# A 16-bit pass moved to GpSimd when it is idle, and the choice of blocks for VectorE, in a scheduled attention kernel

## The chip, the cores and the metric

The kernel runs on one core of one Trainium2 chip. The metric is device time in microseconds of one execution; lower is better. The core has five engines that run their own instruction lists and wait for each other by semaphores: TensorE (PE, matrix products), ScalarE (ACT, here above all exponentials), VectorE (DVE, elementwise work), GpSimd (POOL, elementwise work, no access to PSUM, the accumulators' memory) and SyncE (SP, which issues DMA transfers). SBUF is the core's working memory.

## The reference: what is computed

Four layers work on x, 2048 positions of 512 numbers, each adding its result to x after a layer norm: attention (A), linear attention (B), A, B.

```python
# A: 32 query heads of 16, one key and one value head for all
q = heads(x @ wq); k = x @ wk; v = x @ wv
p = softmax(q k^T * 16**-0.5)
x = x + merge(p v) @ wo
# B: 32 heads of 16, phi(t) = (t + 1 if t > 0 else exp(t)) + 1e-6
kv = sum_s phi(k) v ; z = sum_s phi(k)
x = x + merge(phi(q) kv / (phi(q) z + 1e-6)) @ wo
```

In an A layer the costly part is the exponential of 32 x 2048 x 2048 scores.

## The kernel before

**Blocks.** Scores are made in blocks of 128 keys by 512 columns (128 queries of four heads). A *segment* (class `Seg`, L294) is a query tile `t` (of 16), one of two parities `par`, and a list of key tiles `kts`; it has four blocks (`j` = 0 to 3) for each key tile. The segments of tiles 0 to 3 come in several pieces of few key tiles (`a_segs`, L736); those of tiles 4 to 15 are whole: 16 key tiles, 64 blocks, 24 segments to a layer. A layer has 2048 blocks in all. QK matmuls (L782) write a block's scores to a PSUM bank; the products with V (L836, "PV") add up in one other bank, with four blocks of different `j` side by side; at the end of a segment VectorE copies or adds that bank to `sacc` (L1068, L1070), and `norm` (L1077) transposes and divides it.

**Two ways to the exponential.** ScalarE does most blocks, in groups of two or three (L948, PSUM to `PT`). VectorE does others without an exponential: it adds a constant and writes the result as a 16-bit integer whose bits, read as bfloat16, are near a power of two (L1024, `dve_take`, PSUM to a buffer of `FB`). The first such write alone is coarse, so `NSH` = 4 shifted versions are used, with weights: up to `CHB` = 4 blocks are gathered in one `FB` buffer, a *chunk*, and `dve_shifts` (L1041) makes three further copies with a 16-bit integer added (L1049, SBUF to SBUF, 2048 elements a partition), each in a buffer of its own. PV takes all four, so a block of VectorE's needs four PV matmuls in place of one.

**Who chooses.** `act_stream` (L888) builds ScalarE's groups one after another. For each it asks `dve_split` (the third bank of a group goes to VectorE) or `dve_open` (a free bank goes there). These say no when VectorE's queue is long (`BLS`, `BLO`, `BLT`) or, for a new chunk, when no more than `FBO` = 2 of the `NFB` = 10 buffers are free (`dve_hit`, L996). `dve_pick` (L980) then looks through the running segment and the next four for a block: one of a segment is taken only when more than `CHT` = 12 blocks are left from the running segment up to it (in the last segment `ENDL` = 12) and when more than the share 1 - `DMAX` of its own blocks, one half, is left. `stale` (L975) closes a chunk early when its segment is past or has `CHT // 2` blocks left. `dve_shifts` holds passes of far segments back when few buffers are free (`FBS`, `AHEAD`).

**The order of the work** is written by a planner in Python before the launch (class `Planner`, L36). Each operation has a duration by engine, keys that it reads and writes, and a priority (lower goes first). When an engine is free in the planner's own time, `_dispatch1` (L127) gives it the ready operation with the lowest number; this fixes each engine's instruction list. `backlog` (L104) is the planned time in an engine's queue. `emit` (L274) writes the lists out with semaphore waits for the keys. Thus the durations used for planning shape the order, and on the chip each engine goes through its list in that order, however long things take.

**Others that the change touches.** `ln_tile` (L620) makes the layer norm: statistics on VectorE, `rs` = 1/sqrt on GpSimd (L630), `xn` on VectorE (L633), then a transpose by TensorE or by DMA. `phi` (L1168) makes phi for B layers on ScalarE (L1170) and VectorE (L1171, L1173); its keys go to `pk`, a tile of its own (L398), which `kv_` (L1244) reads. `fill` (L862) and `fill_lin` (L764) put dummy matmuls where TensorE would stand still (L881, L768). `mode` of an operation tells how the TensorE array is split: rows (QK), columns (PV), or full.

Of the kernel before, what the change touches and what calls it, by code (L numbers as in the profile page):

```python
# [6 lines left out]
BF16 = mybir.dt.bfloat16  # L7
# [16 lines left out]


class Op:
    __slots__ = ("eng", "opts", "fn", "deps", "prio", "left", "users", "done", "end", "n", "value", "sem", "signal", "isdma", "name", "freed", "begun", "slot", "cols", "mode")


class Pool_:  # L30
# [5 lines left out]
class Planner:  # L36
# [3 lines left out]
    def __init__(self, nc):  # L40
        self.nc = nc
        self.now = 0.0
        self.events = []
        self.seq = 0
        self.ready = {e: [] for e in ENGS}
        self.busy = {e: False for e in ENGS}
        self.until = {e: 0.0 for e in ENGS}
        self.order = {e: [] for e in ENGS}
        self.writer = {}
        self.readers = {}  # L50
        self.flags = {}
        self.flagwait = {}
        self.level = (0.0, 0.0)
        self.due = []
        self.idle = []
        self.mode = None

    def at(self, t, fn):
        self.seq += 1
# [2 lines left out]
    def ws(self, k):  # L62
        return self.writer.get(k, [])

    def op(self, opts, reads=(), writes=(), prio=5.0, lat=0.08, dma=False, name="", join=None, mode="full"):

        o = Op()
        o.opts, o.prio, o.users, o.done, o.end = opts, prio, [], False, None
        o.eng, o.fn, o.n, o.value, o.sem, o.signal, o.isdma = None, None, None, None, None, False, dma
        o.name = (name, lat)  # L70
        o.freed = False
        o.begun = None
        o.cols = 0
        o.mode = mode
        deps = set()
        for k in reads:
            deps.update(self.ws(k))
        for k in writes:
# [11 lines left out]
        for k in reads:  # L90
# [36 lines left out]
    def _dispatch1(self, e):  # L127
        if self.busy[e]:
            return
        h = self.ready[e]  # L130
        while h:
            _, _, o = heapq.heappop(h)
            if o.eng is not None:
                continue
            dur, fn = o.opts[e]
            if e == PE:
                if self.mode != o.mode:
                    dur += SWITCH
                self.mode = o.mode
            o.eng, o.fn = e, fn  # L140
            self.order[e].append(o)
            self.busy[e] = True
            self.until[e] = self.now + dur
# [6 lines left out]
            return  # L150

    def _freed(self, e, o):
        self.busy[e] = False
# [171 lines left out]
MCRIT = {0: (), 1: (0, 1), 2: (), 3: ()}  # L325
ECRIT = (15,)
WORK = 5000
DMAX = 0.5
RING = 24
NOB = 4  # L330
DTL = 4.0
# [28 lines left out]
CHB = 4  # L360
FBO = 2
FBS = 4
AHEAD = 20
CHT = 12


def bass_interleave_layers__grouped_kv_mqa__linear_attn_block__prompt_kernel(
# [11 lines left out]
    pl = Planner(nc)  # L379
    op = pl.op  # L380
    sb = nc.alloc_sbuf_tensor
# [13 lines left out]
    wo = sb("wo", [P, 4, D], BF16)  # L395
    wqkv = sb("wqkv", [P, FT, 3 * D], BF16)
    wo2 = sb("wo2", [P, 4, D], BF16)
    pk = sb("pk", [P, 8, D], BF16)  # L398
    va = sb("va", [P, 8, H * 17], BF16)
    NXN = 6  # L400
    xn = sb("xn", [P, NXN, D], BF16)
    st = sb("st", [P, T, 2, 6], FP32)
    mv = sb("mv", [P, T, 2], FP32)
    ve = sb("ve", [P, T], FP32)
    rs = sb("rs", [P, T], FP32)
    mhalf = sb("mhalf", [P, 1], FP32)
# [9 lines left out]
    zz = sb("zz", [P, 128], BF16)  # L416
    NPT = 6
    PT = sb("PT", [P, NPT, GA * 512], BF16)
    NFB = 10
    FB = sb("FB", [P, NFB, CHB * 512], BF16)  # L420
    NOS, NOT = 3, 2
    Osb = sb("Osb", [P, NOS, D], BF16)
    OT = sb("OT", [P, NOT, 4, P], BF16)
    rden = sb("rden", [P, 2, 16], FP32)
    sacc = sb("sacc", [P, 8, 512], FP32)
    NAS = 2
    identF = sb("identF", [P, P], FP32)
    NPH = 3
    phE = sb("phE", [P, NPH, D], BF16)
# [47 lines left out]
    def B_(i):  # L477
        return ("bank", i)
# [141 lines left out]
    def ln_tile(t, prio, far=False, crit=False):  # L620
        if t in two:
            two.discard(t)
            n = 2
        else:
            n = 1
# [2 lines left out]
        op({DV: (0.07, lambda e: e.tensor_scalar(out=ve[:, t:t + 1], in0=mv[:, t, 1:2], scalar1=1e-5, scalar2=None, op0=ALU.add))},  # L628
           reads=[("mv", t)], writes=[("ve", t)], prio=prio, lat=0.16)
        op({PO: (0.55, lambda e: e.tensor_tensor(out=rs[:, t:t + 1], in0=ve[:, t:t + 1], in1=mhalf[:], op=ALU.pow))},  # L630
           reads=[("ve", t), "mhalf"], writes=[("rs", t)], prio=prio)
        i = yield ("acq", xn_pool, prio)
        op({DV: (0.325, lambda e: e.tensor_scalar(out=xn[:, i, :], in0=x_sb[:, t, :], scalar1=mv[:, t, 0:1], scalar2=rs[:, t:t + 1],  # L633
                                                op0=ALU.subtract, op1=ALU.mult))},
           reads=[("x", t), ("mv", t), ("rs", t)], writes=[("xn", i)], prio=prio)
        if far:
            o = dmat(xnT[:, :, t * P:(t + 1) * P], xn[:, i, :], [("xn", i)], [("xnT", t)], prio)
            pl.give_after(xn_pool, i, [o])
# [133 lines left out]

    def run_a(L):
        segs = a_segs()
        state = {"si": 0, "done": False, "on": False}

        def qk_reads(sg, kts):
            return [("QT", sg.t)] + [("K", sg.par, kt) for kt in kts]
# [262 lines left out]
        def dve_shifts(blk, f_, hold):  # L1041
            n = 512 * len(blk)
            pr = 8.0 + 0.001 * min(x[0].i for x in blk)
            si = min(x[0].i for x in blk)
            for w in range(1, NSH):
                while len(fb_pool.free) <= FBS and sum(x.total - x.submitted for x in segs[cur["i"]:si]) > (AHEAD if segs[si].blocks < 32 else 0):
                    yield ("sleep", 0.2)
                g_ = yield ("acq", fb_pool, pr)
                o = op({DV: (n / 3840.0 + 0.066, lambda e, w=w, g_=g_: e.tensor_scalar(  # L1049
                    out=FB[:, g_, 0:n].bitcast(I16), in0=FB[:, f_, 0:n].bitcast(I16), scalar1=float(w * 128 // NSH), scalar2=None, op0=ALU.add))},  # L1050
                       reads=[("FB", f_, h) for h in range(len(blk))], writes=[("FB", g_, h) for h in range(len(blk))], prio=pr, lat=0.15)
# [112 lines left out]
    def run_b(L):  # L1164
        def base(t):
            return 1.0 if t >= CRIT else 5.0

        def phi(b, dst, key, pr, n=D, join=None):  # L1168
            i = yield ("acq", ph_pool, pr)
            op({AC: (0.07 + n / 1200.0, lambda e: e.activation(phE[:, i, 0:n], bank(b, n), ACTF.Exp))}, reads=[B_(b)], writes=[("phE", i)], prio=min(pr, 0.9))  # L1170
            op({DV: (0.07 + n / 3840.0, lambda e: e.tensor_scalar(out=phE[:, i, 0:n], in0=phE[:, i, 0:n], scalar1=1.0, scalar2=1e-6, op0=ALU.min, op1=ALU.add))},  # L1171
               writes=[("phE", i)], prio=pr)
            o = op({DV: (0.07 + n / 960.0, lambda e: e.scalar_tensor_tensor(out=dst, in0=bank(b, n), scalar=0.0, in1=phE[:, i, 0:n], op0=ALU.max, op1=ALU.add))},  # L1173
                   reads=[("phE", i)], writes=[B_(b), key], prio=pr, join=join)
            pl.give_after(banks, b, [o])
            pl.give_after(ph_pool, i, [o])
            return o

        def phi_k(t, b, sl, pr):
            yield from phi(b, pk[:, sl, :], ("pk", sl), pr)  # L1180
            pl.flag(("pkin", L, t))

        def crit_k(t, sl, pr):
            bs = yield from acq2(pr)
            for h in range(2):
                mm(bank(bs[h], 256), [(xnT[:, ft, t * P:(t + 1) * P], wqkv[:, ft, D + h * 256:D + h * 256 + 256]) for ft in range(FT)],
                   [("xnT", t), "wqkv"], bs[h], pr + 0.0001 * h, 0.45)
            o = None
            for h in range(2):
                o = yield from phi(bs[h], pk[:, sl, h * 256:h * 256 + 256], ("pk", sl), pr, 256, o)  # L1190
            pl.flag(("pkin", L, t))

        def crit_v(t, sl, pr):
# [50 lines left out]
        def kv_(gi, ts):  # L1244
            pr = base(ts[-1]) + 0.01 * ts[-1] + 0.005
            end = gi == len(KVG) - 1
# [15 lines left out]
            for gs in ((0, 1, 2), (3,)):  # L1262
# [6 lines left out]
                def fn(e, gs=gs, b=b):  # L1269
# [3 lines left out]
                            ins = e.matmul(ps[:, b * 512 + i * 136:b * 512 + (i + 1) * 136], lhsT=pk[:, t % 8, g * P:(g + 1) * P],  # L1273
                                           rhs=va[:, t % 8, g * 136:(g + 1) * 136], start=(not end and t == ts[0]), stop=(t == ts[-1]), skip_group_check=True)
                    return ins
                rd = [("pk", t % 8) for t in ts] + [("va", t % 8) for t in ts]
                o = op({PE: (0.08 * len(gs) * len(ts), fn)}, reads=rd, writes=[B_(b)], prio=pr, lat=0.2)
                o.cols = 136 * len(gs) * len(ts)
                dst = kvacc[:, gs[0] * 136:gs[0] * 136 + n]
# [197 lines left out]
```

## Time and profile before

| what | value |
|---|---|
| time, median of three runs (lowest, highest) | 1580.71 us (1577.74, 1581.18) |
| the profiled execution: its own time | 1583.91 us |
| its span in the profile | 1582.0 us |
| busy: PE, DVE, ACT, POOL | 1474.2, 1372.0, 1509.3, 62.9 us |
| blocks by VectorE (L1024) | 924 of 4096 |
| passes of 2048 elements (L1049) | 693 |
| granted TensorE clock, mean | 0.995 |

The profile is one execution on the chip. A line of a group gives the source line, engine, operation, tiles (out<-in), shapes and count, then busy time in us, mean ns of one, idle time of the engine before them and what ended it ("releaser"). Instructions of an engine overlap a little, so the busy time is less than count times mean. In a timeline a line gives the start and the length in us of a row of like instructions.

### The profile page before, as it was taken

The page shows a single profiled execution, that of the slowest core. Times are in us where ns is not written, and L with a number is a line of the kernel's source. Part 1 is how long each engine was busy: PE and PEld are TensorE (multiplying, and loading weights), DVE is VectorE, ACT ScalarE, POOL GpSimd, SP SyncE. Part 2 cuts the span into 40 slices and gives each one's busy share as a digit, 9 for nine tenths or more (in the row PEclk, how much of TensorE's full clock was granted, in tenths as well). Part 3 has the DMA queues.
Part 4 walks back from the last instruction along what each step waited for, and adds up shares of the span by engine and source line. Part 5 has one row for each costly group of instructions (what it writes and reads, how often), then busy time and mean ns, then how long its engine had stood idle before and what let it go on. Part 6 is the DMA issues. An engine that isn't in the chain of part 4 may idle for free.

```text
span 1582.0 us, 35711 instructions
## 1 busy us (share of the span) xinstructions
PE 1474.2 (93%) x14564; PEld 546.7 (35%) x14667; DVE 1372.0 (87%) x2550; ACT 1509.3 (95%) x1481; POOL 62.9 (4%) x122
## 2 busy tenths in 40 slices
PE   8998999999999999999999999999999999999989
PEld 4432332333333333332644323323333333333335
DVE  7799899999898989997566789999889898998957
ACT  7999999999999999999599999999999999999982
POOL 4000000000000000000011000000000000000000
PEclk9999999999999999999999999999999999999999
DMA  5100000000000000000000000000000000000001
GB/s 128 48 2 1 12 11 12 5 9 7 8 8 8 5 8 5 1 2 1 2 1 1 1 2 15 15 8 8 5 5 8 8 8 8 8 1 2 1 2 54
DMA packets 40433, 17.52 MB, mean 11 GB/s; under 512 B 34128, under 2 KB 39760, under 8 KB 40272
## 3 DMA queue, kind: packets, MB, share of 16 engines
q1 hardware_dynamic: 40272, 15.25, 4.1%
q8 instruction: 117, 1.92, 0.5%
q14 instruction: 44, 0.36, 0.1%
HBM read 5.28 MB, written 2.10 MB: 5 GB/s over the span
## 4 chain that ended last, share of the span: by engine, by line
PE 42%; ACT 36%; DVE 11%; issue 10%; DMA 0%; POOL 0%; SPq 0%; ACTq 0%; DVEq 0%; POOLq 0%
ACT PT L948 35%; PE ps L836 14%; PE ps L782 12%; DVE FB L1024 5%; PE ps L550 4%; PE ps L881 4%; DVE FB L1049 2%; PE ps L707 2%; PE ps L1087 2%; ACT phE L1170 1%; PE ps L768 1%; DVE sacc L1068 1%; DVE st L626 0%; PE ps L1400 0%; PE ps L1381 0%
## 5 line engine op out<-in xcount | busy, mean ns | idle before, releaser
L948 ACT ACTIVATE PT<-ps 128x1024 bf16<-128x1024 f32 (+1 forms) x1350 | 1460.1, 1216 | 13.0 <-PE ps L836 7.2
L1024 DVE TENSOR_SCALAR FB<-ps 128x512 int16<-128x512 f32 x924 | 617.0, 685 | 92.9 <-PE ps L782 88.6
L782 PE MATMUL ps<-QT,KM 32*128 32x512 bf16 x4096 | 529.7, 385 | 51.2 <-ACT PT L948 32.8
L836 PE MATMUL ps<-PT,V 128*32 128x512 bf16 x3172 | 463.5, 388 | 20.3 <-ACT PT L948 17.1
L1049 DVE TENSOR_SCALAR FB<-FB 128x2048 int16<-128x2048 int16 x693 | 451.2, 681 | 2.3 <-PE ps L836 0.5
L836 PE MATMUL ps<-FB,VW 128*32 128x512 bf16 x3696 | 411.1, 384 | 15.7 <-DVE sacc L1068 5.2
L782 PEld LDWEIGHTS ps<-QT,KM 32*128 32x128 bf16 x4096 | 137.9, 91 | 425.4 <-ACT PT L948 188.8
L881 PE MATMUL ps<-QT,V 128*32 128x512 bf16 (+6 forms) x786 | 178.3, 315 | 0.5 <-issue 0.3
L836 PEld LDWEIGHTS ps<-PT,V 128*32 128x32 bf16 x3172 | 116.4, 94 | 156.1 <-ACT PT L948 70.6
L836 PEld LDWEIGHTS ps<-FB,VW 128*32 128x32 bf16 x3696 | 108.6, 94 | 178.2 <-issue 86.3
L630 POOL TENSOR_TENSOR rs<-ve,mhalf 128x1 f32<-128x1 f32 x64 | 45.7, 723 | 1422.3 <-DVE ve L628 1386.0
L881 PEld LDWEIGHTS ps<-QT,V 128*32 128x32 bf16 x786 | 58.9, 95 | 82.0 <-issue 59.6
L550 PE MATMUL ps<-wqkv,xnT 128*128 128x512 bf16 (+1 forms) x218 | 68.1, 369 | 3.0 <-issue 2.1
L1087 PE MATMUL ps<-identF,sacc 128*128 128x128 f32 x256 | 48.6, 293 | 2.9 <-DVE sacc L1068 1.7
L1068 DVE COPY sacc<-ps 128x512 f32<-128x512 f32 x64 | 43.7, 683 | 7.8 <-PE ps L836 7.8
L1170 ACT ACTIVATE phE<-ps 128x512 bf16<-128x512 f32 (+1 forms) x66 | 41.3, 625 | 5.3 <-PE ps L707 3.6
L626 DVE BATCH_NORM_STATS2 st<-x_sb 128x6 f32<-128x512 bf16 x60 | 40.6, 678 | 3.3 <-DMA x_sb<-in_A_x_dram 3.1
L1070 DVE TENSOR_TENSOR sacc<-sacc,ps 128x512 f32<-128x512 f32 x56 | 38.2, 683 | 5.6 <-PE ps L836 4.7
L707 PE MATMUL ps<-xnT,wqkv 128*128 128x128 bf16 x512 | 42.2, 221 | 0.0
L707 PE MATMUL ps<-xnT,wq 128*128 128x128 bf16 x480 | 40.8, 226 | 0.6 <-DMA wq<-in_A_wq_dram 0.6
L550 PEld LDWEIGHTS ps<-wqkv,xnT 128*128 128x128 bf16 x272 | 21.8, 96 | 46.1 <-issue 38.4
L1087 PEld LDWEIGHTS ps<-identF,sacc 128*128 128x128 f32 x256 | 27.4, 140 | 27.4 <-issue 11.1
(114 smaller groups left out, 673.5 us busy)
## 6 DMA issues: line engine op xcount, KB each, us to landing
out_dram<-x_sb SPq DMA_DIRECT2D x16, 128.0 KB, 1.7
x_sb<-in_A_x_dram SPq DMA_DIRECT2D x3, 512.0 KB, 6.9
wqkv<-in_B_wqkv_dram SPq DMA_DIRECT2D x1, 1536.0 KB, 7.3
xnT<-xn SPq DMA_TRANSPOSE x36, 2.4
x_sb<-in_A_x_dram SPq DMA_DIRECT2D x4, 128.0 KB, 2.2
wq<-in_A_wq_dram SPq DMA_DIRECT2D x1, 512.0 KB, 5.0
wo<-in_A_wo_dram SPq DMA_DIRECT2D x1, 512.0 KB, 4.0
wo<-in_B_wo_dram SPq DMA_DIRECT2D x1, 512.0 KB, 8.4
```

The lines of the kernel that those rows point to most:

```text
L550: return e.matmul(dst, lhsT=l, rhs=r, start=(k == 0), stop=(k == len(pairs) - 1))
L630: op({PO: (0.55, lambda e: e.tensor_tensor(out=rs[:, t:t + 1], in0=ve[:, t:t + 1], in1=mhalf[:], op=ALU.pow))}, reads=[("ve", t), "mhalf"] ...
L707: ins = e.matmul(dst[:, g * P:(g + 1) * P], lhsT=lhs(g, k), rhs=rhs(k), start=(k == 0), stop=(k == FT - 1))
L782: return e.matmul(bank(b), lhsT=KM[r, sg.par, kt * P:(kt + 1) * P], rhs=QT[r, sg.t, :], start=True, stop=True)
L836: ins = e.matmul(ps[32 * j:32 * j + 32, ACC * 512:(ACC + 1) * 512], lhsT=V[:, kt, :] if w is None else VW[:, kt, w, :], rhs=ap, start=(k = ...
L881: o = op({PE: (n / 2400.0, lambda e: e.matmul(ps[32 * j:32 * j + 32, b * 512:b * 512 + n], lhsT=V0[:], rhs=QT[:, sg.t, 0:n], start=st, sto ...
L948: ex = op({AC: (0.05 + 0.4267 * n, lambda e, n=n, s_=s_, p_=p_: e.activation(PT[:, p_, 0:n * 512], ps[:, s_ * 512:(s_ + n) * 512], ACTF.Ex ...
L1024: o = op({DV: (0.60, lambda e: e.tensor_scalar(out=dst.bitcast(I16), in0=bank(b), scalar1=VB, scalar2=VLO, op0=ALU.add, op1=ALU.max))}, wr ...
L1049: o = op({DV: (n / 3840.0 + 0.066, lambda e, w=w, g_=g_: e.tensor_scalar(out=FB[:, g_, 0:n].bitcast(I16), in0=FB[:, f_, 0:n].bitcast(I16), ...
L1068: o = op({DV: (0.6, lambda e, src=src: e.tensor_copy(src, bank(ACC)))}, writes=[B_(ACC), key], prio=0.0, lat=0.15)
L1087: o = op({PE: (0.12, lambda e, c=c: e.transpose(ps[:, b * 512 + c * P:b * 512 + (c + 1) * P], src[:, c * P:(c + 1) * P], identF[:]))}, rea ...
L1170: op({AC: (0.07 + n / 1200.0, lambda e: e.activation(phE[:, i, 0:n], bank(b, n), ACTF.Exp))}, reads=[B_(b)], writes=[("phE", i)], prio=min ...
```

## The change

Four things are changed together.

First, an operation can be marked `port`: VectorE's passes (L1049), its `xn` and the first step of `phi` carry the mark, and so does a pass on GpSimd. In the planner, no marked operation starts while another one runs; the engine takes something else from its queue in the meantime. Second, a pass of a full chunk may go to GpSimd: when GpSimd is idle, no other such pass is under way, and VectorE's planned queue is over `PBL` = 0.6 us. While the queue is that long, `dve_shifts` waits for the chunk's last eviction before it decides. `rs` gets a higher priority on GpSimd. Third, `DMAX` goes from 0.5 to 1.0 and `CHT` from 12 to 20, and `FB` has 12 buffers in place of 10; the room comes from `pk`, which now lies in `sacc[2:6]`, with the dependencies for that. Fourth, TensorE, when it would change between columns and full array, goes on with an operation of the present mode if one is ready within `STICK` = 1.5 of the priority.

```diff
-DMAX = 0.5
+DMAX = 1.0
-CHT = 12
+CHT = 20
+PSH = True
+STICK = 1.5
+PBL = 0.6
-    pk = sb("pk", [P, 8, D], BF16)
-    NFB = 10
+    NFB = 12
     sacc = sb("sacc", [P, 8, 512], FP32)
+    pk = sacc[:, 2:6, :].rearrange("p a b -> p (a b)").bitcast(BF16).rearrange("p (s d) -> p s d", d=D)
...
@@ Planner._dispatch1
         while h:
-            _, _, o = heapq.heappop(h)
+            x = heapq.heappop(h)
+            o = x[2]
             if o.eng is not None:
                 continue
             dur, fn = o.opts[e]
+            if o.port and self.port > self.now:
+                held.append(x)
+                continue
+            if e == PE and STICK and o.mode != "row" and o.mode != self.mode != "row":
+                like = [y for y in h if y[2].eng is None and y[2].mode == self.mode and y[0] <= o.prio + STICK]
+                if like:
+                    y = min(like)
+                    h.remove(y)
+                    heapq.heapify(h)
+                    held.append(x)
+                    o = y[2]
+                    dur, fn = o.opts[e]
+            if o.port:
+                self.port = self.now + dur
...
+        for x in held:
+            heapq.heappush(h, x)
+        if held and not self.busy[e] and e != PE:
+            self.at(self.port, lambda: self._dispatch(e))
...
@@ ln_tile: rs, then xn
-           reads=[("ve", t), "mhalf"], writes=[("rs", t)], prio=prio)
+           reads=[("ve", t), "mhalf"], writes=[("rs", t)], prio=prio - 9.0)
...
-           reads=[("x", t), ("mv", t), ("rs", t)], writes=[("xn", i)], prio=prio)
+           reads=[("x", t), ("mv", t), ("rs", t)], writes=[("xn", i)], prio=prio, port=True)
...
@@ dve_shifts
                 g_ = yield ("acq", fb_pool, pr)
-                o = op({DV: (n / 3840.0 + 0.066, lambda e, w=w, g_=g_: e.tensor_scalar(
+                while PSH and len(blk) == CHB and pl.backlog(DV) > PBL and not all(o.done for o in pl.ws(("FB", f_, len(blk) - 1))):
+                    yield ("sleep", 0.1)
+                pool = PSH and len(blk) == CHB and not pl.busy[PO] and state["po"] == 0 and pl.backlog(DV) > PBL
+                if pool:
+                    state["po"] += 1
+                en, du = (PO, n / 1165.0 + 0.25) if pool else (DV, n / 3840.0 + 0.066)
+                o = op({en: (du, lambda e, w=w, g_=g_: e.tensor_scalar(
                     out=FB[:, g_, 0:n].bitcast(I16), in0=FB[:, f_, 0:n].bitcast(I16), scalar1=float(w * 128 // NSH), scalar2=None, op0=ALU.add))},
-                       reads=[("FB", f_, h) for h in range(len(blk))], writes=[("FB", g_, h) for h in range(len(blk))], prio=pr, lat=0.15)
+                       reads=[("FB", f_, h) for h in range(len(blk))], writes=[("FB", g_, h) for h in range(len(blk))], prio=pr, lat=0.15, port=True)
+                if pool:
+                    def gone():
+                        state["po"] -= 1
+                    o.users.append(gone)
...
@@ phi, kv_
-            o = op({DV: (0.07 + n / 960.0, ...)}, reads=[("phE", i)], writes=[B_(b), key], prio=pr, join=join)
+            o = op({DV: (0.07 + n / 960.0, ...)}, reads=[("phE", i)], writes=[B_(b), key], prio=pr, join=join, after=after)
...
-            yield from phi(b, pk[:, sl, :], ("pk", sl), pr)
+            yield from phi(b, pk[:, sl, :], ("pk", sl), pr, after=[("sacc", 2 + sl // 2)])
...
-                rd = [("pk", t % 8) for t in ts] + [("va", t % 8) for t in ts]
+                rd = [("pk", t % 8) for t in ts] + [("va", t % 8) for t in ts] + [("sacc", u) for u in sorted({2 + t % 8 // 2 for t in ts})]
```

The new argument `after` of an operation lists keys that it must come behind, with their readers and writers, without writing them.

More of the change, by code (lines that the diff above doesn't have):

```diff
@@ L26 @@
 class Op:
-    __slots__ = ("eng", "opts", "fn", "deps", "prio", "left", "users", "done", "end", "n", "value", "sem", "signal", "isdma", "name", "freed", "begun", "slot", "cols", "mode")
+    __slots__ = ("eng", "opts", "fn", "deps", "prio", "left", "users", "done", "end", "n", "value", "sem", "signal", "isdma", "name", "freed", "begun", "slot", "cols", "mode", "port")
 class Pool_:
@@ L56, in __init__ @@
         self.mode = None
+        self.port = 0.0
     def at(self, t, fn):
@@ L63, in ws, with op @@
         return self.writer.get(k, [])
-    def op(self, opts, reads=(), writes=(), prio=5.0, lat=0.08, dma=False, name="", join=None, mode="full"):
+    def op(self, opts, reads=(), writes=(), prio=5.0, lat=0.08, dma=False, name="", join=None, mode="full", port=False, after=()):
         o = Op()
@@ L74, in op @@
         o.mode = mode
+        o.port = port
         deps = set()
@@ L77, in op @@
             deps.update(self.ws(k))
-        for k in writes:
+        for k in list(writes) + list(after):
             deps.update(self.ws(k))
@@ L89, in op @@
                 self.readers[k] = []
-        for k in reads:
+        for k in list(reads) + list(after):
             if k not in writes:
@@ L130, in _dispatch1 @@
         h = self.ready[e]
+        held = []
         while h:
-            _, _, o = heapq.heappop(h)
+            x = heapq.heappop(h)
+            o = x[2]
             if o.eng is not None:
@@ L149, in _dispatch1 @@
             self.at(self.now + dur + o.name[1], lambda: self._done(o))
-            return
+            break
+        for x in held:
+            heapq.heappush(h, x)
+        if held and not self.busy[e] and e != PE:
+            self.at(self.port, lambda: self._dispatch(e))
     def _freed(self, e, o):
@@ L774, in run_a @@
         segs = a_segs()
-        state = {"si": 0, "done": False, "on": False}
+        state = {"po": 0, "si": 0, "done": False, "on": False}
         def qk_reads(sg, kts):
@@ L1166, in base, with phi @@
             return 1.0 if t >= CRIT else 5.0
-        def phi(b, dst, key, pr, n=D, join=None):
+        def phi(b, dst, key, pr, n=D, join=None, after=()):
             i = yield ("acq", ph_pool, pr)
@@ L1171, in phi @@
             op({DV: (0.07 + n / 3840.0, lambda e: e.tensor_scalar(out=phE[:, i, 0:n], in0=phE[:, i, 0:n], scalar1=1.0, scalar2=1e-6, op0=ALU.min, op1=ALU.add))},
-               writes=[("phE", i)], prio=pr)
+               writes=[("phE", i)], prio=pr, port=True)
             o = op({DV: (0.07 + n / 960.0, lambda e: e.scalar_tensor_tensor(out=dst, in0=bank(b, n), scalar=0.0, in1=phE[:, i, 0:n], op0=ALU.max, op1=ALU.add))},
-                   reads=[("phE", i)], writes=[B_(b), key], prio=pr, join=join)
+                   reads=[("phE", i)], writes=[B_(b), key], prio=pr, join=join, after=after)
             pl.give_after(banks, b, [o])
@@ L1189, in crit_k @@
             for h in range(2):
-                o = yield from phi(bs[h], pk[:, sl, h * 256:h * 256 + 256], ("pk", sl), pr, 256, o)
+                o = yield from phi(bs[h], pk[:, sl, h * 256:h * 256 + 256], ("pk", sl), pr, 256, o, [("sacc", 2 + sl // 2)])
             pl.flag(("pkin", L, t))
```

## The prediction

> **What bounds the kernel now.** I first read the table by stretches, cut where the costliest groups change. Columns: stretch and length, then busy time and instruction count of PE, its weight loads, VectorE, ScalarE and GpSimd, then TensorE's granted clock.
>
> ```profile
> 80.00:720.00 640.00, 596.56 (x5887) 203.81 (x5928) 586.68 (x1042) 635.73 (x613) 13.16 (x14) 1.00 0.03 6
> 754.00:895.00 141.00, 134.66 (x1393) 68.51 (x1403) 95.47 (x229) 124.88 (x132) 15.77 (x33) 1.00 0.01 2
> 895.00:1510.00 615.00, 576.59 (x5645) 194.45 (x5685) 564.66 (x1009) 609.92 (x590) 13.43 (x15) 1.00 0.03 7
> ```
>
> The two long stretches, the attention layers, hold 1255 of 1582 us. ScalarE is busy 99% of them, VectorE 92%, GpSimd 2%. TensorE's 93% holds dummy matmuls (L881, 178.3 us), so it has room. ScalarE's exponentials set the time, and the question is how many blocks VectorE can take off them. The groups, by cost:
>
> ```profile
> L948 ACT ACTIVATE PT<-ps 128x1024 bf16<-128x1024 f32 (+1 forms) x1350 | 1460.1, 1216 | 13.0 <-PE ps L836 7.2
> L1024 DVE TENSOR_SCALAR FB<-ps 128x512 int16<-128x512 f32 x924 | 617.0, 685 | 92.9 <-PE ps L782 88.6
> L1049 DVE TENSOR_SCALAR FB<-FB 128x2048 int16<-128x2048 int16 x693 | 451.2, 681 | 2.3 <-PE ps L836 0.5
> ```
>
> VectorE takes 924 of 4096 blocks: four evictions (L1024) and three 16-bit passes (L1049) to a full chunk, 231 chunks. Start to start, one of either takes 0.60 us (its 0.68 overlaps the next), so a block costs VectorE 4 x 0.60 / 4 + 3 x 0.60 / 4 = 1.05 us. ScalarE's exponential of two blocks starts 0.91 us before the next, of three 1.33 (medians of the trace), so a block taken out of a group of three saves 0.43 us.
>
> How GpSimd and VectorE get on is seen in the tiny `rs` (L630), without passes nearby and among them; the four durations are minimum, median, maximum:
>
> ```profile
> L630 POOL TENSOR_TENSOR rs<-ve,mhalf x17: 547/548/550, 762.6 to 879.2; 128x1 f32<-128x1 f32 x17
> L630 POOL TENSOR_TENSOR rs<-ve,mhalf x15: 548/925/1466, 976.0 to 1503.8; 128x1 f32<-128x1 f32 x15
> ```
>
> Beside two 16-bit passes in a row it lasts until both are over (GpSimd's line last):
>
> ```profile
> 460.11 1.29 DVE L1049 TENSOR_SCALAR FB<-FB 128x2048 int16<-128x2048 int16 x2
> ...
> 460.28 1.16 POOL L630 TENSOR_TENSOR rs<-ve,mhalf 128x1 f32<-128x1 f32 x1 [37.14 <-DVE ve L628]
> ```
>
> At 551.75, beside an L1024, it takes 0.55. So a VectorE pass from SBUF to SBUF holds GpSimd off, an eviction from PSUM does not.
>
> **Part by part.**
>
> *The pass on GpSimd.* It goes there where GpSimd is free and VectorE has over 0.6 us queued. No row shows a GpSimd pass of 2048 elements. Below: the plain memset's slope, 0.20 us for 128 elements and 0.31 for 256, gives 0.31 + 1792 x 0.86 ns = 1.85 us. Above: VW, a tensor_tensor, takes 0.40 for 128; less the 0.10 of a one-element memset that is 2.33 ns an element, 4.9 us in all. A pass has one stream in and one out, no second operand: nearer to the memset, so I take 2.0.
>
> The Trainium skill (GPSIMD Engine Reference, section 3.1) gives 1.03 cycles an element where only the ports bind and 2.6 with two inputs, at 1.2 GHz; by it 128 elements of two inputs take 0.28 us, which with the 0.10 agrees with VW's 0.40, and a pass would take some 1.9 us, an estimate from that page. The sum would be the same.
>
> VectorE saves 0.60 per such pass. But while GpSimd holds on, VectorE's own passes and `xn` cannot run; the planner's new port mark holds them back. In the trace I looked at the 2.0 us after each chunk's fourth eviction: VectorE spends 1.25 us of them on work of the other kind, so on average 0.75 would be idle and the pass would lose 0.15. But in 175 of the 231 chunks there is at least 0.75 us of such work, 1.49 on average, and these are the ones with a queue, which the new test picks: +0.09 as things stand, +0.60 if additional evictions fill the rest. I take 0.35 and 175 passes: 61 us of VectorE.
>
> *Two more buffers; current segment.* DMAX 1.0 and CHT 20 let VectorE take blocks of the running segment down to 20 left, where it now goes over to the next at half. A chunk for a later segment keeps its buffers until TensorE reaches it; so the new buffers and the nearer choice let more chunks be open. VectorE's gaps in 120–720 and 920–1515 are 50 + 46 = 96 us, nearly all waits for L782 of a block taken late. Bounds 0 and two thirds (64); I take a third, 32.
>
> Sum: 61 + 32 = 93 us of VectorE. A further block costs it 1.05, and the shorter stage takes 0.92 x 0.43 = 0.40 us from it: 93 / 1.45 = 64 blocks, x 0.43 = **28 us**. TensorE gets 3 x 64 more PV matmuls, 48 groups of four at 0.33 (chain of waits), 16 us, against 178 us of dummies.
>
> *Layer ends.* Here half a segment (32 blocks) is ScalarE's alone, as VectorE may not pass half and there is no next segment:
>
> ```profile
> 739.90 15.37 ACT L948 ACTIVATE PT<-ps 128x1536 bf16<-128x1536 f32 x12 [0.23 <-PE ps L836]
> ...
> 756.58 0.58 DVE L1285 TENSOR_TENSOR kvacc<-kvacc,ps 128x408 f32<-128x408 f32 x1 [14.71 <-PE ps L1273]
> ```
>
> Now VectorE goes on to 12 left: of some 20 blocks a third, 7 x 0.43 = 3.0, less 0.5 for its own last passes: 2.5 a layer, **5 us**.
>
> *What it costs.* A chunk that goes stale at 10 left is passed on partly filled: at most one for each of 48 full segments, 3 passes with some 0.1 us of fixed cost: 14 us of VectorE at worst, 4 of time; I take 1. PV matmuls of a late GpSimd pass stall TensorE now and then: I take 4. Together **5**. `rs` goes ahead of passes in GpSimd's queue but waits up to 2.0 us for a running one, 30 times in these stretches; behind it `xn` and its DMA transpose in SP's queue. These feed the next layer, up to hundreds of us away, and VectorE's queue hides them: 0; with that cover gone 30 x 2 = 60. The sticking of TensorE to one tile mode reorders full-array work and PV: no row prices a switch; between -2 and +2 for the chain's pieces between modes, I take 0. `pk` inside `sacc` waits for norms of units 2 to 5, long past; 0, at most a layer's wait of some 2.
>
> Total: 1583.9 (the profiled execution's own time, span 1582.0) - 28 - 5 + 5 = 1555.9. It stood 3.2 above the median 1580.7, so **1553**.
>
> **Rivals.**
>
> *Late at TensorE (slower).* The program has no wait that enforces the port mark: VectorE can start its own pass first, and GpSimd's then starts 0.4 to 0.9 us late (`rs`: median 0.38 over, at most 0.92); or the pass is dearer than 2.0. TensorE works in its written order: the PV (L836) for that pass waits, behind it the next QK (L782), and behind that ScalarE. What hides it is one exponential, 0.91 us, less a QK of 0.39: 0.5 us. Each pass later by X costs X - 0.5. The gains of 33 over 175 passes are 0.19, so from X = 0.7 it is slower: a pass of 2.7 us. X = 0.9: 175 x 0.4 - 33 = +37, 1618. X = 1.2: 1670. For it: nothing in the trace shows such a pass, and the memset does no arithmetic. Against: evictions follow most fourth evictions, and they don't hold GpSimd off.
>
> *The port eats it.* 175 x (0.60 - 0.75) = -26, with the 32 of the buffers 6 us of VectorE, 4 blocks, 2 us; ends and costs cancel: 1579, no change. The Trainium skill (SBUF — State Buffer, "SBUF: two separate sides") says that the port pair shared by the two is an exclusive lock held for a whole instruction and the loser waits; the `rs` rows agree for GpSimd as loser, and `xn` (0.64 beside a VW, 0.41 alone) hints at the other way. By that rule alone this rival would hold if VectorE had no other work.
>
> *Full cover.* 231 passes at 0.60 plus 64: 203 / 1.45 = 140 blocks, 60 us, with the ends 65: 1516.
>
> *Few passes (doesn't do what it says).* VectorE's queue must be over 0.6 us from the moment a chunk closes until its last eviction is done; the first pass often starts only 0.24 us after it. With hardly any: 32 / 1.45 x 0.43 = 9, with ends 14: 1566.
>
> **Chances.** Forecast 0.40, full cover 0.16, few passes 0.14, port eats it 0.07, late at TensorE 0.23. A measurement of this kernel tells 0.2% (3 us, the spread of its three runs) from no change. Faster 0.70, same 0.07, slower 0.23. The range takes in most of the full cover and the milder half of the late case: 1520 to 1605.
>
> **What would show it.** In the changed profile: L1049's successor has a GpSimd group of 128x2048, 120 to 230 times, mean 1.9 to 2.3 us; L1024's count rises from 924 to some 990, exponentials of three blocks become fewer; the 14.7 us gap of VectorE at the layer's end shrinks. ScalarE still at 98% or more of the long stretches: forecast; L836 waiting tens of us for GpSimd, and ScalarE for L782: the slower rival. It is wrong if GpSimd's pass is much over 2.7 us, or if VectorE's own passes grow far beyond 0.68.

## The result and the profile after

The change makes the kernel slower by 43%: 2263.47 us (median of four runs, 2262.67 to 2266.32) against 1580.95 for the kernel before; ratio 1.432, 95% interval 1.430 to 1.435. Forecast were 1553 and a range up to 1605.

The same stretches as before, in the changed kernel's table (columns as before, the last two the DMA engines' busy share and GB/s; the stretches are cut at the new layer bounds):

```profile
80.00:1100.00 1020.00, 736.75 (x6153) 220.21 (x6194) 918.38 (x1068) 668.49 (x646) 558.13 (x114) 0.81 0.02 4
1110.00:1260.00 150.00, 141.50 (x1462) 69.72 (x1469) 99.82 (x236) 133.48 (x137) 15.61 (x33) 1.00 0.01 1
1290.00:2170.00 880.00, 654.92 (x5407) 195.77 (x5451) 800.09 (x942) 585.86 (x569) 475.81 (x98) 0.81 0.02 5
```

All the loss lies in the attention stretches: from a layer's first exponential to its last they take 361 and 320 us longer, of 680 in the span. The B stretch between them is as it was. ScalarE, busy 99% there before, is now busy 66%. The groups of the changed kernel, with GpSimd's new one:

```profile
L973 ACT ACTIVATE PT<-ps 128x1024 bf16<-128x1024 f32 (+1 forms) x1354 | 1459.4, 1152 | 662.8 <-PE ps L807 596.6
L1080 POOL TENSOR_SCALAR FB<-FB 128x2048 int16<-128x2048 int16 x192 | 1063.2, 5544 | 869.8 <-DVE FB L1049 543.2
L1080 DVE TENSOR_SCALAR FB<-FB 128x2048 int16<-128x2048 int16 (+2 forms) x582 | 918.0, 1599 | 1.2 <-PE ps L861 0.2
L1049 DVE TENSOR_SCALAR FB<-ps 128x512 int16<-128x512 f32 x1028 | 683.8, 683 | 154.7 <-PE ps L807 150.2
```

Three readings. GpSimd's pass takes 5.54 us on average (at least 5.36), where 2.0 was forecast and the planner had 2.01. VectorE's own passes (same line, L1080) rose from 681 to 1599 ns on average, while its evictions (now L1049) kept 683. And ScalarE stands still for 663 us, before 13, 597 of it for QK matmuls (L807). How the three hang together is seen in a few microseconds of the changed kernel's timeline, VectorE first, then GpSimd, TensorE and ScalarE (start, length, instruction, idle time before):

```profile
620.46 0.24 DVE L1129 RECIPROCAL rden<-ps 128x16 f32<-128x16 f32 x1
620.63 5.08 DVE L1080 TENSOR_SCALAR FB<-FB 128x2048 int16<-128x2048 int16 x1
625.63 0.41 DVE L1133 TENSOR_TENSOR Osb<-ps,rden 128x256 bf16<-128x256 f32 x1
```

```profile
614.03 11.14 POOL L1080 TENSOR_SCALAR FB<-FB 128x2048 int16<-128x2048 int16 x2 [1.04 <-DVE xn L658]
```

```profile
625.76 0.62 PE L861 MATMUL ps<-FB,VW 128*32 128x512 bf16 x4 [3.80 <-DVE FB L1080]
...
626.74 0.61 PE L807 MATMUL ps<-QT,KM 32*128 32x512 bf16 x3
```

```profile
621.12 1.45 ACT L973 ACTIVATE PT<-ps 128x1536 bf16<-128x1536 f32 x1 [1.67 <-PE ps L807]
627.45 1.45 ACT L973 ACTIVATE PT<-ps 128x1536 bf16<-128x1536 f32 x1 [4.88 <-PE ps L807]
```

GpSimd is in two passes in a row until 625.17. A VectorE pass that starts at 620.63 stands until 625.71, 0.54 us after GpSimd's end: about the 0.60 us that a pass takes from start to start. TensorE's next PV (L861) needs this pass and waits 3.80 us for it; the QK (L807) behind that PV in TensorE's order waits too, and ScalarE for the QK, 4.88 us. Over the whole kernel TensorE's longest waits are these (who for whom, us in total, times, longest; before, the largest was 32.8 us, for ScalarE):

```profile
PE ps L861 <- DVE FB L1080: 181.8, 69, 8.1
PE ps L807 <- DVE FB L1049: 111.7, 52, 7.5
PE ps L861 <- POOL FB L1080: 90.9, 43, 4.8
```

PVs wait for VectorE's late passes, QKs for evictions, which can stand behind such a pass in VectorE's order (one at 619.87 does, behind a pass of 3.30 us), and PVs for GpSimd's own passes. Taking for each VectorE pass, `xn` and first step of `phi` what it lasted beyond its usual 0.69, 0.42 and 0.29 us, 186 instructions were held off for **620 us**, beside a loss of 683. Whether the one makes the other is what the experiments try.

### The profile page after: what moved, and what is told of

The parts are those of the page before. It is cut to its first block, busy times and chain, and to the rows that moved or that the text cites. A ratio compares the mean times of both kernels' runs of the same rounds, so it can differ in the third digit from the quotient of the medians.

```text
span 2261.6 us, 36288 instructions
## 1 busy us (share of the span) xinstructions
PE 1699.5 (75%) x14636; PEld 565.4 (25%) x14747; DVE 1988.5 (88%) x2536; ACT 1516.4 (67%) x1492; POOL 1127.4 (50%) x314
## 5 line engine op out<-in xcount | busy, mean ns | idle before, releaser
L1080 POOL TENSOR_SCALAR FB<-FB 128x2048 int16<-128x2048 int16 x192 | 1063.2, 5544 | 869.8 <-DVE FB L1049 543.2
L1080 DVE TENSOR_SCALAR FB<-FB 128x2048 int16<-128x2048 int16 (+2 forms) x582 | 918.0, 1599 | 1.2 <-PE ps L861 0.2
L861 PE MATMUL ps<-FB,VW 128*32 128x512 bf16 x4112 | 658.0, 469 | 251.7 <-DVE FB L1080 133.4
L1049 DVE TENSOR_SCALAR FB<-ps 128x512 int16<-128x512 f32 x1028 | 683.8, 683 | 154.7 <-PE ps L807 150.2
L807 PE MATMUL ps<-QT,KM 32*128 32x512 bf16 x4096 | 595.8, 435 | 142.4 <-DVE FB L1049 111.7
L861 PE MATMUL ps<-PT,V 128*32 128x512 bf16 x3068 | 605.0, 438 | 83.8 <-DVE FB L1080 48.3
L807 PEld LDWEIGHTS ps<-QT,KM 32*128 32x128 bf16 x4096 | 137.8, 92 | 620.3 <-issue 252.2
L861 PEld LDWEIGHTS ps<-FB,VW 128*32 128x32 bf16 x4112 | 146.3, 102 | 513.8 <-DVE FB L1080 164.4
L861 PEld LDWEIGHTS ps<-PT,V 128*32 128x32 bf16 x3068 | 134.6, 98 | 212.7 <-issue 84.0
L906 PE MATMUL ps<-QT,V 128*32 128x512 bf16 (+6 forms) x554 | 143.5, 348 | 9.7 <-DVE FB L1049 5.9
L658 DVE TENSOR_SCALAR xn<-x_sb,mv,rs 128x512 bf16<-128x512 bf16 x64 | 74.1, 1164 | 8.2 <-POOL rs L655 7.1
L1206 DVE TENSOR_SCALAR phE<-phE 128x512 bf16<-128x512 bf16 (+1 forms) x66 | 55.8, 845 | 6.6 <-ACT phE L1205 6.5
L1205 ACT ACTIVATE phE<-ps 128x512 bf16<-128x512 f32 (+1 forms) x66 | 39.1, 592 | 25.7 <-PE ps L732 14.7
```

Source lines behind the costliest of these rows:

```text
L807: return e.matmul(bank(b), lhsT=KM[r, sg.par, kt * P:(kt + 1) * P], rhs=QT[r, sg.t, :], start=True, stop=True)
L861: ins = e.matmul(ps[32 * j:32 * j + 32, ACC * 512:(ACC + 1) * 512], lhsT=V[:, kt, :] if w is None else VW[:, kt, w, :], rhs=ap, start=(k = ...
L906: o = op({PE: (n / 2400.0, lambda e: e.matmul(ps[32 * j:32 * j + 32, b * 512:b * 512 + n], lhsT=V0[:], rhs=QT[:, sg.t, 0:n], start=st, sto ...
L1049: o = op({DV: (0.60, lambda e: e.tensor_scalar(out=dst.bitcast(I16), in0=bank(b), scalar1=VB, scalar2=VLO, op0=ALU.add, op1=ALU.max))}, wr ...
L1080: o = op({en: (du, lambda e, w=w, g_=g_: e.tensor_scalar(out=FB[:, g_, 0:n].bitcast(I16), in0=FB[:, f_, 0:n].bitcast(I16), scalar1=float(w ...
```

## The experiments

Time of the kernel before beside these runs: 1580 to 1583 us.

**prices: what a pass costs.**

> A kernel of its own: it copies x to the output and leaves out the whole computation. GpSimd runs passes alone, two of each: int16 add of a constant over 2048, 1024 and 512 elements, a bfloat16 and a float32 multiply over the same bytes, a copy, a 32-bit integer add with a broadcast second operand over 1024 words, a bfloat16 add of two tensors, a memset. Then one int16 pass of 2048 beside a row of eight VectorE operations of one kind: its own 16-bit pass, an eviction from PSUM, an add of two SBUF tensors, bn_stats from SBUF. Theory 'price' (the pass itself costs 5.4 us, not 2.0): 5.3 to 5.5 us for 2048 int16 alone, and in proportion 2.7 and 1.4 for 1024 and 512. Rival 'contention' (2.0 us alone, stretched in the kernel by VectorE): 1.9 to 2.2 alone, over 4 only beside VectorE. Beside it, both expect VectorE's 16-bit passes to stand still until the GpSimd pass ends and the PSUM evictions to keep 0.6 us.

Measured, in groups of this kernel (L30 holds three sizes: shortest, median and longest in ns; below it count, busy us, mean ns):

```profile
L30 POOL TENSOR_SCALAR dst<-src x6: 1487/2768/5367, 2.8 to 20.9; 128x2048 int16<-128x2048 int16 x2, 128x1024 int16<-128x1024 int16 x2, 128x512 int16<-128x512 int16 x2
```

```profile
L33 POOL TENSOR_SCALAR dst<-src 128x2048 bf16<-128x2048 bf16 x2 | 10.7, 5364 | 0.2
L37 POOL TENSOR_TENSOR dst<-src 128x2048 bf16<-128x2048 bf16 x2 | 7.2, 3598 | 0.2
L34 POOL TENSOR_SCALAR dst<-src 128x1024 f32<-128x1024 f32 x2 | 5.5, 2768 | 0.2
L35 POOL COPY dst<-src 128x2048 bf16<-128x2048 bf16 x2 | 3.8, 1891 | 0.1
L36 POOL TENSOR_TENSOR dst<-src,cst 128x1024 int32<-128x1024 int32 x2 | 3.8, 1890 | 0.2
L38 POOL MEMSET dst<- 128x2048 bf16 x2 | 3.6, 1804 | 0.1
```

Alone, the 16-bit pass takes 5.37 us: it is dear by itself, and 'contention' is out. An operation with a constant costs (5367 - 2768) / 1024 = 2.54 ns an element in all three types tried (int16, bfloat16, float32); a copy of the same bytes 1.89 us, a memset 1.80. So one stream in and one out is cheap, but the operation with a constant is not. The Trainium skill (GPSIMD Engine Reference, section 3.1) gives 1.03 cycles an element where the ports bind, by an estimate at its 1.2 GHz 0.86 ns; that is near the copy (0.92 ns) and far from the pass, so the 1.9 us that the prediction estimated from that page is wrong for the pass. A 32-bit add, of two 16-bit numbers at a time, takes 1.89 us for the same 2048.

Beside it:

```profile
58.08 10.84 DVE L43 TENSOR_SCALAR dsu<-dsv 128x2048 int16<-128x2048 int16 x8 [54.51 <-POOL dst L38]
58.94 5.79 POOL L70 TENSOR_SCALAR dst<-src 128x2048 int16<-128x2048 int16 x1 [1.00 <-DVE dsu L43]
...
68.95 5.77 DVE L44 TENSOR_SCALAR dsu<-ps 128x512 int16<-128x512 f32 x8
69.80 5.36 POOL L70 TENSOR_SCALAR dst<-src 128x2048 int16<-128x2048 int16 x1 [5.07 <-DVE dsu L44]
...
75.27 6.95 DVE L45 TENSOR_TENSOR dsu<-dsv 128x512 bf16<-128x512 bf16 x8 [0.54 <-POOL dst L70]
75.85 5.53 POOL L70 TENSOR_SCALAR dst<-src 128x2048 int16<-128x2048 int16 x1 [0.69 <-DVE dsu L45]
```

Eight VectorE passes beside a GpSimd pass take 10.84 us, some 5 more than their own; eight evictions from PSUM 5.77, nothing more, and eight bn_stats 5.80, nothing more either. GpSimd's pass, 5.37 us alone, takes 5.79 where it starts during a VectorE pass. For these passes the rule of the Trainium skill that the prediction named (SBUF — State Buffer, "SBUF: two separate sides": one engine holds the shared port pair for a whole instruction) agrees with the trace in both directions. For the add of two SBUF tensors (L45) it agrees only in part: one add took 3.74 us in place of 0.43, but it ended 1.4 us before the end that the trace gives for GpSimd's pass, and further adds ran beside the rest of it.

**no_pool: the change without the pass on GpSimd.**

```diff
-PSH = True
+PSH = False
```

> All of the change but the pass on GpSimd: every pass is VectorE's. Theory 'price': the rest of the change is harmless, 1545 to 1575 us, VectorE taking more blocks than before. Rival 'the rest' (current segment, buffers, sticking to a tile mode or pk inside sacc break the order): over 2000.

Measured: 1557.10 us, ratio to before 0.985 (0.984 to 0.987). The rest of the change is a gain of 1.5%; 'the rest' is out. VectorE's evictions against those of before: 1017 blocks in place of 924, and the wait for late QK down from 88.6 us to 20.7.

```profile
L1049 DVE TENSOR_SCALAR FB<-ps 128x512 int16<-128x512 f32 x1017 | 673.3, 683 | 23.5 <-PE ps L807 20.7
```

**short_pass: the price as forecast.** (The cut leaves out the memsets that fill the buffers once at the start.)

```diff
...
+                m = 736 if pool else n
-                    out=FB[:, g_, 0:n].bitcast(I16), in0=FB[:, f_, 0:n].bitcast(I16), ...
+                    out=FB[:, g_, 0:m].bitcast(I16), in0=FB[:, f_, 0:m].bitcast(I16), ...
```

> The changed kernel with its written order, but GpSimd's pass does only 736 of the 2048 elements, so that it lasts about 2.0 us as planned; the rest of that buffer keeps what it held before (the buffers are set once at the start), so the weights of those blocks are not the reference's. Theory 'price' (all the loss comes from 5.4 us where 2.0 were planned): 1540 to 1590. Rival 'order' (VectorE overtakes the port mark, and a pass of 2.0 us loses too): over 1650.

Measured: 1572.62 us, ratio 0.995 (0.993 to 0.997); GpSimd's pass took 2.28 us on average. With a pass near the planned length the changed kernel is not slow: nearly all of the loss needs the length. But it is 15 us behind no_pool: even so, GpSimd's passes gained nothing.

**true_price: the planner is told.**

```diff
-                en, du = (PO, n / 1165.0 + 0.25) if pool else ...
+                en, du = (PO, n / 400.0 + 0.25) if pool else ...
```

> The changed kernel, but the planner is told 5.37 us for GpSimd's pass (n / 400 + 0.25) in place of 2.01; it writes a new order, with some 130 passes on GpSimd. Theory 'price, through the order': with the right figure the engines no longer wait for each other out of turn, 1640 to 1720, still slower than before, since the port mark holds VectorE's own passes off for 5.4 us at a time. Rival 'price, through the lock alone' (the loss is the blocked VectorE time, whatever the order): over 2000.

Measured: 1929.25 us, ratio 1.220 (1.216 to 1.225), 127 passes. This lies between both expectations: a miss. I set each VectorE instruction of the profile beside its place in the planner's own order. Of 264 us for which marked instructions were held off, 224 lay on instructions that the planner had put *ahead* of the GpSimd pass that held them off. Nothing in the program makes GpSimd wait for them: it waits only for its data and its buffer, so where VectorE is behind its plan GpSimd starts first and has the ports for 5.4 us. I call this overtaking; the prediction had thought of it only the other way round.

**true_ordered: a wait for the port mark.** (With the price of true_price.)

```diff
...
             if o.port:
                 self.port = self.now + dur
+                if e == PO and self.last is not None:
+                    o.deps.add(self.last)
+                if e == DV:
+                    self.last = o
```

> As true_price (1929; the planner knows of 5.37 us), with one wait more for each GpSimd pass: it also waits for the last VectorE instruction with the port mark that the planner had put ahead of it. Theory 'overtaking': on the chip GpSimd starts ahead of VectorE passes that were planned before it and holds them off for its whole length (224 of 265 us of blocked time in true_price were on such passes); with the wait that is gone: 1640 to 1780. Rival 'length alone' (it is the time that the pair of ports is taken, in whatever order): 1880 to 1950.

Measured: 1664.86 us, ratio 1.052 (1.049 to 1.055): 264 us less than true_price, by one wait for each pass. 'Overtaking' is borne out; time held off on instructions planned ahead of the pass fell from 224 us to 0, and all time held off from 264 us to 82.

**dummy_port: passes that nobody reads.**

```diff
-PSH = True
+PSH = False
...
-    fb_pool = Pool_(range(NFB))
+    fb_pool = Pool_(range(NFB - 1))
...
+                if w == 1 and len(blk) == CHB and not pl.busy[PO] and pl.backlog(DV) > PBL:
+                    op({PO: (5.37, lambda e: e.tensor_scalar(
+                        out=FB[:, NFB - 1, :].bitcast(I16), in0=FB[:, NFB - 1, :].bitcast(I16), scalar1=0.0, scalar2=None, op0=ALU.add))},
+                       writes=["scr"], prio=5.0, lat=0.15)
```

> The kernel without passes on GpSimd (the run no_pool, 1557), but GpSimd gets 117 passes of 2048 elements and 5.4 us, where a full chunk's first pass is due and VectorE has a queue, that add 0 to a buffer that nothing else reads (the twelfth of FB; the chunks have eleven, which costs up to 10 us). No one waits for them. Theory 'held off' (the loss is VectorE's own SBUF passes standing still behind GpSimd's): VectorE's blocked passes lengthen as in the changed kernel (some 3 us for each GpSimd pass there), 117 x 2 to 3 = 230 to 350 us more: 1790 to 1920. Rival 'late products' (the loss is TensorE waiting in its order for GpSimd's result): no one reads it, so 1555 to 1580.

Measured: 2122.36 us, ratio 1.341 (1.336 to 1.345). 'Late products' is out as the necessary cause: without one reader, 116 passes cost 565 us over no_pool. Some of that may be the buffer that the chunks lack: the run rest_10buf, below, lacks two and is 30 us behind no_pool. The size was missed: 4.9 us a pass, not 2 to 3. These passes wait for no data, so GpSimd ran up to five of them in a row between its `rs`, and held VectorE's passes and `xn` off for most of each row. The products that TensorE then lacks are VectorE's own (last line, of TensorE's waits):

```profile
L1085 DVE TENSOR_SCALAR FB<-FB 128x2048 int16<-128x2048 int16 x738 | 876.6, 1213 | 1.4
L1050 DVE TENSOR_SCALAR FB<-ps 128x512 int16<-128x512 f32 x986 | 655.2, 684 | 89.4 <-PE ps L808 85.2
L1081 POOL TENSOR_SCALAR FB<-FB 128x2048 int16<-128x2048 int16 x116 | 652.1, 5622 | 7.0
L659 DVE TENSOR_SCALAR xn<-x_sb,mv,rs 128x512 bf16<-128x512 bf16 x64 | 123.7, 1937 | 7.0 <-POOL rs L656 5.9
...
PE ps L862 <- DVE FB L1085: 296.6, 69, 14.0
```

**int_pass and int_ordered: the pass as a 32-bit add, without and with the wait.**

(`wadd` is a small tile with the constants, set once at the start.)

```diff
...
+                def add(e, w=w, g_=g_):
+                    return e.tensor_tensor(out=FB[:, g_, 0:n].bitcast(I32), in0=FB[:, f_, 0:n].bitcast(I32), in1=wadd[:, w - 1:w].to_broadcast([P, n // 2]), op=ALU.add)
-                o = op({en: (du, lambda e, w=w, g_=g_: e.tensor_scalar(
+                o = op({en: (du, add if pool else lambda e, w=w, g_=g_: e.tensor_scalar(
...
```

> The changed kernel, with GpSimd's pass as a 32-bit integer add over 1024 words of two 16-bit numbers each, the constant from a small tile read with step 0 (1.93 us alone in the run of prices, where the 16-bit form took 5.37). The result is the same number for number. Theory 'price': the loss is gone with the length: 1545 to 1580. Rival 'order' (any pass on GpSimd costs more than it saves by far): over 1650.

> As int_pass, with the wait of true_ordered. Theory 'overtaking': at 1.9 us little VectorE time is blocked out of turn (11 us in short_pass), so 3 to 12 us less than int_pass. Rival 'length alone': the same as int_pass or up to 5 us more for the waits.

Measured: int_pass 1625.09 us, ratio 1.026 (1.023 to 1.030); int_ordered 1557.19, ratio 0.983 (0.980 to 0.987). GpSimd's pass took 2.02 us on average in the one, 1.89 in the other, and still int_pass is outside both expectations: with the length right, overtaking alone costs 68 us, far more than the 3 to 12 expected. The time held off falls by as much, from 105 to 38 us. The expectation took 11 us held off out of turn from short_pass; counted as in true_price it is 32 of 50 us there, and 79 of 105 in int_pass. short_pass, with passes no shorter, is only 15 us behind no_pool; its planned order is another (192 passes on GpSimd against 189), and what in it makes the difference was not tried.

```profile
L1085 POOL TENSOR_TENSOR FB<-FB,wadd 128x1024 int32<-128x1024 int32 x189 | 380.8, 2019 | 927.0 <-DVE FB L1053 491.9 <-PE ps L865 230.7 <-PE ps L811 106.1
```

```profile
L1090 POOL TENSOR_TENSOR FB<-FB,wadd 128x1024 int32<-128x1024 int32 x189 | 357.9, 1894 | 916.3 <-DVE FB L1091 364.7 <-DVE FB L1058 261.9 <-PE ps L870 157.6
```

In the second (int_ordered) GpSimd's largest idle time ends with VectorE's own pass (L1091): the new wait at work.

**after_ordered: the changed kernel with the wait alone.** (The edit is that of true_ordered.)

> The changed kernel, its written order and its 5.37 us passes kept, with only the wait of true_ordered added (each GpSimd pass also waits for the last marked VectorE instruction that the planner had put ahead of it). In the changed kernel's profile 310 us of blocked VectorE time lay on passes planned ahead of the GpSimd pass that blocked them, 313 us on passes planned behind it. Theory 'two halves' (overtaking and length each cost about half): 1850 to 2000. Rival 'overtaking is all': 1560 to 1700. Rival 'length is all': over 2150.

Measured: 2141.18 us, ratio 1.356 (1.353 to 1.359). Overtaking was worth 122 of the 683 us, less than the half that I expected, and the time held off fell by about as much, from 620 to 492 us; 'length is all' is nearer, though it too missed by 9 us. With nothing overtaken any more, these 492 us lie on instructions that the planner put behind a GpSimd pass it believed over after 2.0 us; and TensorE now waits 159 us for GpSimd's results themselves, before 91:

```profile
PE ps L866 <- POOL FB L1085: 159.1, 71, 4.8
PE ps L812 <- DVE FB L1054: 83.6, 57, 4.5
PE ps L866 <- DVE FB L1085: 80.6, 53, 4.0
```

(TensorE's waits in after_ordered: who for whom, us in total, times, longest.)

**rest_10buf and rest_oldpick: which part of the rest gains.** (Both with `PSH = False`, as no_pool.)

```diff
-    NFB = 12
+    NFB = 10
```

```diff
-DMAX = 1.0
-CHT = 20
+DMAX = 0.5
+CHT = 12
```

> The run no_pool (1557) with 10 buffers in place of 12. Theory 'buffers': the two buffers carry most of the gain of 26 us over the kernel before, 1572 to 1588. Rival 'choice' (keeping to the current segment carries it): 1552 to 1565.

> The run no_pool (1557) with the old choice of blocks (DMAX 0.5, CHT 12) and 12 buffers. Theory 'buffers': 1557 to 1568. Rival 'choice': 1575 to 1590. If both this run and the one with 10 buffers fall in between or above, the two work only together.

Measured: 1587.02 us with 10 buffers, ratio 1.005 (1.003 to 1.006); 1583.98 with the old choice, ratio 1.003 (1.002 to 1.004). Each alone gives nothing, or a little less than that; together they give some 25 us. In a group of VectorE's evictions it is seen why the first has no effect: with 10 buffers 922 blocks, as many as before, and 90 us of waits for QK; with 12 buffers and the old choice 953; with both 1017.

```profile
L1049 DVE TENSOR_SCALAR FB<-ps 128x512 int16<-128x512 f32 x922 | 615.3, 684 | 93.9 <-PE ps L807 90.4
```

**int_more: more passes on GpSimd.** (PBL 0.3 in int_ordered.)

> The run int_ordered (1557) with PBL 0.3 in place of 0.6, so that GpSimd takes more passes (217 in place of 189). Theory 'VectorE's time still counts': 1548 to 1556. Rival 'the pair of ports eats it' (what VectorE saves it stands still again): 1556 to 1570.

Measured: 1554.51 us, ratio 0.984 (0.982 to 0.986), with 217 passes. The time lies in the range of 'VectorE's time still counts', but the interval overlaps that of int_ordered and of no_pool: the three can't be told apart.

## Why the prediction was wrong, point by point

| kernel | time, us | GpSimd passes | mean of one, us | VectorE held off, us |
|---|---|---|---|---|
| no_pool | 1557 | 0 | | 0 |
| int_more | 1555 | 217 | 1.90 | 39 |
| int_ordered | 1557 | 189 | 1.89 | 38 |
| short_pass | 1573 | 192 | 2.28 | 50 |
| int_pass | 1625 | 189 | 2.02 | 105 |
| true_ordered | 1665 | 127 | 5.37 | 82 |
| true_price | 1929 | 127 | 5.54 | 264 |
| dummy_port | 2122 | 116 | 5.62 | 511 |
| after_ordered | 2141 | 192 | 5.39 | 492 |
| changed kernel | 2263 | 192 | 5.54 | 620 |

("Held off" is counted as in the section on the result, over all marked VectorE instructions.)

*"A pass has one stream in and one out, no second operand: nearer to the memset, so I take 2.0."* This is the step that failed. The pass takes 5.37 us alone and 5.54 in the kernel, beyond even the upper bound of 4.9, and both signs of being wrong that the prediction named came: a pass far over 2.7 us, and VectorE's own passes far beyond 0.68 (1599 ns on average). The memset's row says nothing of an operation with a constant; VW, the only elementwise arithmetic of GpSimd in the trace at a size, gave 2.33 ns an element, near the 2.54 measured. And the bound of 4.9 that I had worked out did not go into the range: by my own formula it gives X = 2.9 and 1581 - 33 + 175 x 2.4 = 1968 us.

*"Late at TensorE": each pass costs X - 0.5, slower from 2.7 us on.* The side was right, and so was the end of the path: a PV that lacks its pass, the QK behind it, then ScalarE. With X = 3.37 the formula gives some 2050 us; measured were 2263. What it left out is that VectorE's own passes come late too, held off by GpSimd's. TensorE waits 182 us for those, 112 for evictions (3 before), and 91 for GpSimd's results, the only one of the three that the formula has. dummy_port shows that holding VectorE off is enough for a loss of that kind: there no one reads GpSimd's results.

*"VectorE can start its own pass first, and GpSimd's then starts late."* It goes the other way: GpSimd starts ahead of VectorE passes that were planned before it. In the changed kernel 310 us of the time held off were of this kind; one wait for each pass takes 122 us off the time there, 264 in true_price and 68 in int_pass.

*The pass saves 0.35 us net, 61 us of VectorE.* With the right length and the wait (int_ordered) the kernel is as fast as without any pass on GpSimd: 1557.2 against 1557.1. The rival "the port eats it" is right here in that the passes gain nothing, but only partly in why. GpSimd's 189 passes save VectorE some 113 us (at 0.60). Held off it is for 38, and it waits 39 us more than in no_pool for a late QK (59.2 against 20.7), so that it takes only 8 blocks more (1025 against 1017). So saved VectorE time did not become blocks as the sum had it; why the QKs come later was not traced.

```profile
L1058 DVE TENSOR_SCALAR FB<-ps 128x512 int16<-128x512 f32 x1025 | 682.2, 684 | 63.8 <-PE ps L816 59.2
```

*Buffers and current segment, 32 us of VectorE; layer ends, 5 us; together with the passes 33 us of time.* Without any pass on GpSimd these parts give some 25 us (1582.1 for the kernel before on the same chip, 1557.1 for no_pool). VectorE takes 93 blocks more than before, with three partly filled passes of 1536 elements and three of 1024. Of its waits for late QK 68 us went away (88.6 to 20.7), where I had taken 32 and 64 as the upper bound. At the prediction's 0.43 us a block 93 blocks would be 40 us; where the other 15 went was not traced. The row of 12 exponentials at the first layer's end, with VectorE idle for 14.7 us, is now 5, with 3.0 (the end of the layer in no_pool, ScalarE, then VectorE):

```profile
729.44 6.47 ACT L973 ACTIVATE PT<-ps 128x1536 bf16<-128x1536 f32 x5
```

```profile
736.40 0.69 DVE L1103 COPY sacc<-ps 128x512 f32<-128x512 f32 x1 [3.03 <-PE ps L861]
```

rest_10buf and rest_oldpick show that buffers and choice don't add up as separate terms: only together do they gain. `pk` inside `sacc`, the moved `rs` and the sticking of TensorE to one tile mode were costed at nothing; no_pool holds all three and still gains, but they were not tried one by one.

Not settled: why GpSimd's operation with a constant takes 2.54 ns an element, and how much of the loss is TensorE's lower clock, which came with its standing still.

## What to carry to other kernels

Price an operation on an engine by a row of the same operation, and where there is none, run it alone first: a single short run would have shown 5.4 us and a 32-bit form at 1.9. A pass moved to GpSimd does not run beside VectorE's 16-bit SBUF passes or `xn`, only beside work such as evictions from PSUM; count how much of that VectorE has in the meantime before counting a gain. An exclusion that exists only in a planner's mind needs a wait on the chip, or the engine that runs ahead takes the resource out of turn.

## What the runs showed of the hardware

GpSimd's cost hangs on the kind of operation far more than on bytes: for 4096 bytes a partition a 16-bit add of a constant took 5.37 us, a float32 multiply 2.77, an add of a bfloat16 tensor to itself 3.60, a copy 1.89, a 32-bit integer add with a broadcast operand 1.89. A VectorE pass that was held off until the end of GpSimd's pass ended 0.54 to 0.55 us after it, all 150 of those that lasted over 1.5 us in the changed kernel, so it went on at once. And TensorE's granted clock, 0.995 on average before, fell to 0.81 in the attention stretches of the changed kernel, where TensorE was busy 72 and 74%, and stayed at 1.00 in the B stretch at 94%; its QK matmuls went from 385 to 435 ns.
